# W_down's first 256 rows on 32 partitions, half by SyncE's queue and half by GpSimd's

## The chip, the core and the metric

The kernel runs on one core of one Trainium2 chip. A core has five engines with instruction streams of their own (TensorE, written PE in the profile, with PEld for its weight loads; VectorE, DVE; ScalarE, ACT; GpSimd, POOL; SyncE, SP) and 16 DMA engines that move data between HBM and the on-chip memory of 128 partitions. The metric is device time in microseconds (us) of one execution. Before the change it is 195.08 us, the median of three runs (195.07 to 195.08).

## What is computed

One decode step of a transformer block for 4 tokens: a layer norm, then attention over a window of 4096 cached positions and, beside it, a SwiGLU feed-forward network, both added to the input.

```python
xn = layernorm(x)                                    # 4 x 512
q = xn @ wq                                          # 32 heads of 128
k, v = k_cache[:, :, Sk-4096:], v_cache[:, :, Sk-4096:]   # 8 kv heads, 4 query heads share one
p = softmax(q @ k.T * 128**-0.5)
a = (p @ v) @ wo                                     # 4096 -> 512
g = silu(xn @ w_gate); u = xn @ w_up                 # 512 -> 1792
out = x + a + (g * u) @ w_down                       # 1792 -> 512
```

All tensors are bf16. The window of the two caches is 64 MiB; wq and wo are 4 MiB each; w_gate, w_up and w_down 1.75 MiB each.

## The kernel before

The work goes by kv heads: eight groups, each with one 4 MiB load of K and one of V. K and V have two buffers each (`KB`, `VB`). For a group PE transposes K in 16 chunks (L415), DVE and ACT copy the transposes out of PSUM (L326, L280), PE computes scores (L427), maxima are found and subtracted (L434, L439), ACT takes the exponential (L283), and PE multiplies by V (L448) and by ones for the softmax denominator (L454). `spin` (L470) puts idle matmuls where PE would otherwise wait.

All bulk loads go through SP's queue, in the order in which `on_sync` (L235 to L267) issues them: wq, w_gate, w_up, then K and V of each group, then W_down, then wo. A load is issued ahead of its need as soon as its buffer comes free: K of group g waits for the transposes of group g-2 (L239), V for the product with V of group g-2 (L250). Wo overwrites the first K buffer, so its five pieces (`WOS`: 16, 8, 5, 2 and 1 rows of 32 per partition) wait for the last transposes that read it (L264). A DMA queue has a ring on each DMA engine, and a load of 128 partitions is split over the 16 DMA engines, eight partitions to each.

The feed-forward part is done at both ends. At the start PE computes gate and up (L396) for F = 1792 columns in NM + NX pieces: NM = 13 pieces of 128 columns, and NX = 8 pieces that hold the first 128 columns in another split, 16 (`JX`) at a time. At the end `down` (L482) multiplies the 13 pieces of 128 rows by `WD`, and `down_rest` (L487) the 8 pieces of 16 rows by `WDX`. `WD` holds W_down's rows 128 to 1791, 13 rows to a partition. `WDX` holds rows 0 to 127 on 16 partitions, eight rows (8 KB) to a partition; it lies in the first 16 partitions of `WG`, w_gate's buffer, whose last reader is the gate product. `WDX` is loaded by four transfers (L263); transfer o writes partitions o, o+4, o+8 and o+12:

```python
wdx_ap = B_w_down[0:F - FM].rearrange("(i o m) n -> o i m n", o=4, m=NX)   # L185
eng.dma_start(WDX[o:JX:4], wdx_ap[o]).then_inc(d_wd, 16)                   # L263
```

After `down` and `down_rest`, PE adds x (L532) and multiplies by wo as its pieces land (L534 to L544); rows 0 to 15 accumulate in four column groups (L474), which ACT copies out (L298), and the rest in two (L478). DVE and ACT copy the result (L370, L300), and ACT's queue stores it (L302).

GpSimd makes constants at the start (`on_gpsimd`, L191 to L233): identity matrices, masks, and `sel`, a 128 x 32 matrix with a one where row and column agree modulo 32, made by four selections with a drain behind each of the last three (L226). It signals `s_go` (L202), for which ACT waits, and `s_const` (L233), for which PE waits, and issues no DMA.

Of the kernel before, what the change touches and what calls it, by code (L numbers as in the profile page):

```python
# [3 lines left out]
BF16 = mybir.dt.bfloat16  # L4
FP32 = mybir.dt.float32
ALU = mybir.AluOpType
# [4 lines left out]
def bass_parallel_sum__sliding_block_cached__swiglu_ffn__decode_kernel(  # L11
# [15 lines left out]
    F = B_w_gate.shape[1]  # L27
# [3 lines left out]
    NF = F // 128  # L31
# [16 lines left out]
    WOE = 16  # L48
    NR = HQ * Dh // 128

    NM = NF - 1
    FM = 128 * NM
    NX = 8
    JX = 128 // NX

    def sb(name, shape, dtype, align=32):
        return nc.alloc_sbuf_tensor(name, shape, dtype, align_bytes=align)
# [8 lines left out]
    WU = sb("wu_sb", [128, NC, F], BF16, 512)  # L66
    WD = sb("wd_sb", [128, NM, D], BF16, 512)
    WO = KB[0][:].rearrange("p t d -> p (t d)").rearrange("p (r n) -> p r n", r=NR)

    WDX = WG[0:JX].rearrange("p c f -> p (c f)")[:, 0:NX * D].rearrange("p (m n) -> p m n", n=D)  # L70
    X = sb("x_sb", [B, D], BF16, 512)
# [24 lines left out]
    S2 = sb("s2", [128, D], FP32)  # L96
    ex = sb("ex", [128, NM + NX, B], FP32)
    gs = sb("gs", [128, NM + NX, B], FP32)
    guT = sb("guT", [128, NM + NX, 32], BF16)
    ident = sb("ident", [128, 128], BF16)  # L100
# [6 lines left out]
    dq = sb("dq", [128, 4], FP32)  # L107
    dr = sb("dr", [128, NR], BF16)
    sel = sb("sel", [128, 32], FP32)
    head = sb("head", [128, 128], FP32)  # L110
    y = sb("y_sb", [B, D], BF16)

    ps = nc.alloc_psum_tensor
# [13 lines left out]
    q_ps = ps_S[0][:, 0:HQ * B]  # L127
    gate_ps = ps_O[:, 64:64 + (NM + NX) * B].rearrange("p (t b) -> p t b", b=B)
    up_ps = ps_O[:, 192:192 + (NM + NX) * B].rearrange("p (t b) -> p t b", b=B)
# [6 lines left out]
    def sem(name):  # L136
        return nc.alloc_semaphore(name=name)
# [2 lines left out]
    d_wg = sem("d_wg")  # L140
    d_wu = sem("d_wu")
    d_wd = sem("d_wd")
    d_out = sem("d_out")
    d_wo = [sem("d_wo%d" % q) for q in range(len(WOS) - 1)]
    d_k = [sem("d_k%d" % s) for s in range(2)]
# [10 lines left out]
    s_gu = sem("s_gu")  # L156
# [25 lines left out]
    wg_ap = B_w_gate.rearrange("(p c) n -> p c n", c=NC)  # L182
    wu_ap = B_w_up.rearrange("(p c) n -> p c n", c=NC)
    wd_ap = B_w_down[F - FM:F].rearrange("(p t) n -> p t n", t=NM)
    wdx_ap = B_w_down[0:F - FM].rearrange("(i o m) n -> o i m n", o=4, m=NX)  # L185
    wo_ap = A_wo.rearrange("(p r) n -> p r n", r=NR)

    def kv_ap(cache, g, a, b):
        return cache[:, g, Sk - W:, :].rearrange("b (j t) d -> j b t d", j=NJ)[:, :, a:b, :]

    def on_gpsimd(eng):  # L191
        eng.memset(ident[:], 0.0)
        eng.memset(I4[:], 0.0)
        eng.memset(st_eps[:], EPS)
        eng.memset(ones[:], 1.0)
        eng.memset(own[:], 1.0)
        eng.memset(moff[:], 0.0)
        eng.memset(coff[:], 0.0)
        eng.memset(neg[:], 0.0)
        eng.memset(dq[:], 1.0)  # L200
        eng.memset(sel[:], 0.0)
        eng.drain().then_inc(s_go, 1)  # L202

        def select(t, pattern, op, fill, base, mult):
            eng.affine_select(t, t, pattern=pattern, compare_op=op, fill=fill, base=base,
                              channel_multiplier=mult)

        def rows(n):
            select(sel[:], [[-1, 32]], ALU.not_equal, 1.0, -32 * n, 1)
        select(I4[:], [[-1, B]], ALU.not_equal, 1.0, 0, 1)  # L210
        select(ident[:], [[-1, 128]], ALU.not_equal, 1.0, 0, 1)
        select(neg[:], [[-1, NH]], ALU.not_equal, -1.0, 0, 1)
        ownv = own[:].rearrange("k (j b) -> k j b", b=B)
        moffv = moff[:].rearrange("k (j b) -> k j b", b=B)
        coffv = coff[:].rearrange("k (b h) -> k b h", h=REP)
        select(ownv, [[0, NJ], [-REP, B]], ALU.is_ge, 0.0, 0, 1)
        select(moffv, [[0, NJ], [-REP, B]], ALU.is_ge, OFF, 0, 1)
        select(coffv, [[-REP, B], [0, REP]], ALU.is_ge, OFF, 0, 1)
        select(dq[:], [[-32, 4]], ALU.is_ge, 0.0, 0, 1)
        rows(0)  # L220
        eng.drain()
        select(ownv, [[0, NJ], [REP, B]], ALU.is_ge, 0.0, REP - 1, -1)
        select(moffv, [[0, NJ], [REP, B]], ALU.is_ge, OFF, REP - 1, -1)
        select(coffv, [[REP, B], [0, REP]], ALU.is_ge, OFF, REP - 1, -1)
        select(dq[:], [[32, 4]], ALU.is_ge, 0.0, 31, -1)
        for n in range(1, 4):  # L226
            rows(n)
            eng.drain()
        eng.tensor_copy(dr[:], sel[:])
        eng.tensor_copy(head[:], sel[:, 0:1].to_broadcast([128, 128]))  # L230
        eng.memset(dsum[:], 1.0)
        eng.memset(Osb[:], 0.0)
        eng.drain().then_inc(s_const, 1)  # L233

    def on_sync(eng):  # L235
        def load(g):
            u = g % 2
            if g >= 2:
                eng.wait_ge(s_tr[NCH - 1], g - 1)  # L239
            if g < HKV - 1:  # L240
                eng.dma_start(KB[u][:], kv_ap(A_k_cache, g, 0, NT)).then_inc(d_k[u], 16)
            else:

                H = NT // 2
                eng.dma_start(KB[u][:, 0:H], kv_ap(A_k_cache, g, 0, H)).then_inc(d_k[u], 16)
                eng.dma_start(KB[u][:, H:], kv_ap(A_k_cache, g, H, NT)).then_inc(d_kh, 16)
            if g == 1:
                eng.wait_ge(s_q, 1)
            if g >= 2:
                eng.wait_ge(s_pv, g - 1)  # L250
            eng.dma_start(VB[u], kv_ap(A_v_cache, g, 0, NT)).then_inc(d_v[u], 16)

        def load_wo(n, a, b):
            eng.dma_start(WO[:, a:b, :], wo_ap[:, a:b, :]).then_inc(d_wo[n], 16)

        eng.dma_start(WQ, wq_ap).then_inc(d_wq, 16)
        eng.dma_start(WG[:], wg_ap).then_inc(d_wg, 16)
        eng.dma_start(WU[:], wu_ap).then_inc(d_wu, 16)
        for g in range(HKV):
            load(g)  # L260
        eng.dma_start(WD[:], wd_ap).then_inc(d_wd, 16)
        for o in range(4):
            eng.dma_start(WDX[o:JX:4], wdx_ap[o]).then_inc(d_wd, 16)  # L263
        eng.wait_ge(s_tr[NCH - 1], HKV - 1)  # L264
        for q in range(len(WOS) - 1):
            load_wo(q, WOS[q], WOS[q + 1])
        eng.wait_ge(d_out, 16)  # L267
# [104 lines left out]
    def on_tensor(eng):  # L372
# [100 lines left out]
        def acc4(n, left, right, start, stop):  # L473
            return mm(acc4_ps[32 * n:32 * n + 32, :], left, right, start=start, stop=stop, skip_group_check=True)  # L474
# [10 lines left out]
                acc4(t % 4, guT[:, t, :], WD[:, t, :], t < 4, False)  # L485

        def down_rest():  # L487
            for m in range(NX):
                acc4(m % 4, guT[0:JX, NM + m, :], WDX[:, m, :], False, False)

        with eng.Fori(1, HKV + 1, 2) as m:

            d = eng.snap((m - 1) * 8 + 16)
            for u in range(2):
                n = m if u == 0 else eng.snap(m + 1)
# [31 lines left out]
        for b in range(B):  # L527
            last = mm(perm_ps[b // 2][:, NR * (b % 2):NR * (b % 2 + 1)], OT[:, b, 2:HKV + 2].rearrange("p k h q -> p (k h q)"), dr[:])
        last.then_inc(s_pm, 1)
        down_rest()  # L530
        spin(2, 1)
        acc(ident[0:B, 0:B], X[:], True, False)  # L532
# [15 lines left out]


    on_sync(nc.sync)  # L550
    on_gpsimd(nc.gpsimd)
    on_scalar(nc.scalar)
    on_vector(nc.vector)
# [28 lines left out]
```

## Time and profile before

| | |
|---|---|
| median of three runs | 195.08 us |
| the profiled execution | 195.3 us |
| its span, first to last instruction | 193.9 us |
| bytes moved | 81.14 MB, mean 418 GB/s |
| PE busy (matmul) | 163.8 us |
| DVE, ACT, POOL busy | 99.0, 69.1, 5.7 us |
| mean granted TensorE clock | 0.991 |

All times of the trace are counted from the span's start. In rows of the timeline the columns are start, duration, engine (a q behind it is its sequencer or DMA queue), source line, operation, output <- inputs, shapes and count; in brackets the idle time before it and what ended that. In tables by windows, "DMA share" is the busy share of the 16 DMA engines in that stretch.

### The profile page before, as it was taken

How to read it: one execution, taken by the hardware profiler on the slowest of the kernel's cores; microseconds unless marked ns; L12 is line 12 of the kernel's file. 1: busy time of each engine (PE TensorE's matmuls, PEld its weight loads, DVE VectorE, ACT ScalarE, POOL GpSimd, SP SyncE). 2: the span in 40 equal slices, each digit the busy share in tenths (PEclk: the TensorE clock that was granted, in tenths of full speed). 3: DMA queues.
4: the chain of work that ended last, by engine and by line, in shares of the span. 5: the costliest groups of instructions: out<-in, count | busy, mean ns of one | idle time of the engine just before them, and what ended most of it. 6: DMA issues, size and time to landing. Idle time of an engine off the chain costs nothing.

```text
span 193.9 us, 6951 instructions
## 1 busy us (share of the span) xinstructions
PE 163.8 (84%) x3179; PEld 135.2 (70%) x3179; DVE 99.0 (51%) x200; ACT 69.1 (36%) x100; POOL 5.7 (3%) x33
## 2 busy tenths in 40 slices
PE   0038973998699899999999799989996999999995
PEld 0038973997389759956994699469945994997532
DVE  0200011578258737870885188428842884588230
ACT  5510000243416343525461446234623462363421
POOL 7300000000000000000000000000000000000000
PEclk9999999999789999999999999999999999999999
DMA  6999999999999999999999999999999999999993
GB/s 216 433 438 429 427 429 433 429 433 429 433 429 436 426 429 436 426 433 433 439 433 433 433 433 433 433 433 433 433 433 433 433 426 433 439 433 433 436 400 131
DMA packets 3800, 81.14 MB, mean 418 GB/s; under 512 B 440, under 2 KB 576, under 8 KB 832
## 3 DMA queue, kind: packets, MB, share of 16 engines
q1 hardware_dynamic: 3776, 81.00, 97.5%
q8 instruction: 8, 0.13, 0.2%
q10 hardware_dynamic: 16, 0.01, 0.0%
HBM read 81.01 MB, written 0.00 MB: 418 GB/s over the span
## 4 chain that ended last, share of the span: by engine, by line
PE 48%; DMA 44%; DVE 5%; issue 1%; SPq 1%; ACT 0%; DVEq 0%
DMA kbuf<-in_A_k_cache_dram 44%; PE ps_kt L415 23%; PE ps_s L427 8%; PE ps_o L448 5%; PE ps_kt L470 4%; DVE kT L326 2%; PE ps_s L439 2%; PE ps_s L464 2%; DVE mx L332 2%; PE ps_s L478 1%; PE ps_s L474 1%; PE ps_s L461 1%; PE ps_kt L454 1%; PE ps_kt L434 0%; ACT s L298 0%
## 5 line engine op out<-in xcount | busy, mean ns | idle before, releaser
L415 PE MATMUL ps_kt<-ident,kbuf 128*128 128x128 bf16 x1024 | 78.2, 224 | 9.0 <-DMA kbuf<-in_A_k_cache_dram 8.5
L415 PEld LDWEIGHTS ps_kt<-ident,kbuf 128*128 128x128 bf16 x1024 | 60.6, 100 | 11.2 <-DMA kbuf<-in_A_k_cache_dram 9.6
L326 DVE COPY kT<-ps_kt 128x1024 bf16<-128x1024 bf16 x88 | 57.6, 686 | 18.5 <-PE ps_kt L415 16.5
L280 ACT ACTIVATE kT<-ps_kt 128x1024 bf16<-128x1024 bf16 x40 | 40.9, 1023 | 52.9 <-PE ps_kt L415 52.9
L427 PE MATMUL ps_s<-qC,kT 128*128 128x16 bf16 x1024 | 44.8, 170 | 2.6 <-DVE kT L326 1.9
L427 PEld LDWEIGHTS ps_s<-qC,kT 128*128 128x128 bf16 x1024 | 38.4, 97 | 4.6 <-DVE kT L326 4.1
L283 ACT ACTIVATE p<-ps_s 128x512 bf16<-128x512 f32 x32 | 16.5, 603 | 34.0 <-PE ps_s L439 34.0
L332 DVE TENSOR_REDUCE mx<-ps_s 128x16 f32<-128x512 f32 x32 | 22.0, 689 | 6.9 <-PE ps_s L427 5.0
L470 PE MATMUL ps_kt<-own,ones 128*128 128x512 bf16 x82 | 20.7, 380 | 0.0
L448 PE MATMUL ps_o<-vbuf,p 128*32 128x256 bf16 x512 | 19.1, 289 | 0.3
L448 PEld LDWEIGHTS ps_o<-vbuf,p 128*32 128x32 bf16 x512 | 14.9, 101 | 5.9 <-ACT p L283 4.2
L343 DVE TENSOR_REDUCE dsum<-ps_kt 128x16 f32<-128x256 f32 x8 | 3.4, 425 | 28.6 <-PE ps_kt L454 28.6
L454 PE MATMUL ps_kt<-p,ones 128*32 128x256 bf16 x64 | 16.9, 287 | 0.0
L470 PEld LDWEIGHTS ps_kt<-own,ones 128*128 128x128 bf16 x82 | 6.6, 97 | 7.0 <-issue 1.1
L377 PE MATMUL ps_s<-i,xn 4*128 4x4 f32 x4 | 0.6, 254 | 10.1 <-DVE xn L312 10.1
L439 PE MATMUL ps_s<-cm,own 128*128 128x512 bf16 x32 | 8.3, 380 | 1.0 <-DVE cm L340 1.0
L377 PEld LDWEIGHTS ps_s<-i,xn 4*128 4x128 f32 x4 | 0.6, 208 | 10.1 <-issue 10.1
L454 PEld LDWEIGHTS ps_kt<-p,ones 128*32 128x32 bf16 x64 | 6.6, 103 | 0.1
L290 ACT ACTIVATE ex<-ps_o 128x84 f32<-128x84 f32 x1 | 0.2, 240 | 17.5 <-PE ps_o L396 17.5
L439 PEld LDWEIGHTS ps_s<-cm,own 128*128 128x128 bf16 x32 | 2.5, 97 | 5.3 <-DVE cm L340 3.4
L286 ACT ACTIVATE osb<-ps_o 128x256 f32<-128x256 f32 x8 | 3.1, 383 | 8.2 <-PE ps_kt L454 8.2
L464 PE MATMUL ps_s<-sel,osb 128*128 128x16 f32 x36 | 5.8, 275 | 0.0
(83 smaller groups left out, 84.8 us busy)
## 6 DMA issues: line engine op xcount, KB each, us to landing
vbuf<-in_A_v_cache_dram SPq DMA_DIRECT2D x8, 4096.0 KB, 30.5
kbuf<-in_A_k_cache_dram SPq DMA_DIRECT2D x7, 4096.0 KB, 27.4
vbuf<-in_A_wq_dram SPq DMA_DIRECT2D x1, 4096.0 KB, 12.4
kbuf<-in_A_k_cache_dram SPq DMA_DIRECT2D x2, 2048.0 KB, 25.3
kbuf<-in_A_wo_dram SPq DMA_DIRECT2D x1, 2048.0 KB, 27.2
wg_sb<-in_B_w_gate_dram SPq DMA_DIRECT2D x1, 1792.0 KB, 16.1
wu_sb<-in_B_w_up_dram SPq DMA_DIRECT2D x1, 1792.0 KB, 20.9
wd_sb<-in_B_w_down_dram SPq DMA_DIRECT2D x1, 1664.0 KB
```

The source lines that it names most:

```text
L280: eng.activation(KT[:, c % 4], kt_ps[c % 3], ACT.Copy).then_inc(s_ev[c], 1)
L283: eng.activation(P[:, BT * q:BT * (q + 1), :], ps_S[q][:].rearrange("p (t n) -> p t n", n=NH), ACT.Exp, scale=SCALE).then_inc(s_p[q], 1)
L326: eng.tensor_copy(KT[:, c % 4], kt_ps[c % 3]).then_inc(s_ev[c], 1)
L332: eng.tensor_reduce(mx[:, q, :], ps_S[q][:].rearrange("p (t n) -> p n t", n=NH), AX.X, ALU.max)
L343: eng.tensor_reduce(dsum[:], den_ps.rearrange("p (t n) -> p n t", n=NH), AX.X, ALU.add).then_inc(s_dn, 1)
L415: last = eng.transpose(kt_ps[c % 3][:, k, :], KB[u][:, CH * c + k, :], ident[:])
L427: last = mm(ps_S[q][:, NH * t:NH * (t + 1)], KT[:, c % 4, k, :], QC[:], start=(t == 0), stop=False, skip_group_check=True)
L439: mm(ps_S[q][:].rearrange("p (t n) -> p t n", n=NH), own[:], CM[:].unsqueeze(1).to_broadcast([128, BT, NH]), start=False, stop=True, skip_ ...
L448: mm(O_ps[32 * n:32 * n + 32, :], P[:, t:t + 2, :].rearrange("p t n -> p (t n)"), VB[u][:, t:t + 2, :].rearrange("p t d -> p (t d)"), star ...
L454: last = mm(den_ps[32 * n:32 * n + 32, :], ones[:, 0:32], P[:, DT * e:DT * (e + 1), :].rearrange("p t n -> p (t n)"), start=(e < 4), stop= ...
L464: last = mm(O2_ps, Osb[:, Dh * h:Dh * (h + 1)], sel[:, NH * h:NH * (h + 1)], start=(h == 0), stop=(h == 1), skip_group_check=True)
L470: mm(ps_kt[k][:], ones[:], own[:].unsqueeze(1).to_broadcast([128, 4, 128]), skip_group_check=True)
```

## The change

W_down's first 256 rows, not the first 128, are taken out of the 128-partition tile. `WD` has 12 rows to a partition and `WDX` 32 partitions with eight rows each. SP's four transfers load `WDX`'s partitions 0 to 15, now four neighbouring partitions each (0 to 3, 4 to 7, and so on); four transfers on GpSimd's queue load partitions 16 to 31 in the same way. Ahead of each of these GpSimd issues a transfer of twelve short rows, each of two pieces of 32 bytes, into a tile `pad` that nothing reads. GpSimd issues its eight transfers once the gate and up products are done (`s_gu`), because `WDX` lies in w_gate's buffer, and PE waits for all eight (`d_wx`) ahead of `down_rest`. `sel` is made by two additions of halves of the identity matrix instead of a memset and four selections.

```diff
-    NM = NF - 1
+    NM = NF - 2
     FM = 128 * NM
     NX = 8
-    JX = 128 // NX
+    JX = 256 // NX
...
+    sel2 = sb("sel2", [128, 64], FP32)
     head = sb("head", [128, 128], FP32)
+    pad = sb("pad", [12, 4, 2, 16], BF16)
...
-    wdx_ap = B_w_down[0:F - FM].rearrange("(i o m) n -> o i m n", o=4, m=NX)
+
+    wdx_ap = B_w_down[0:F - FM].rearrange("(o i m) n -> o i m n", i=4, m=NX)
...
-        eng.memset(sel[:], 0.0)
         eng.drain().then_inc(s_go, 1)
...
-        rows(0)
-        eng.drain()
+        eng.drain()
+
+        eng.tensor_tensor(sel2[:], ident[:, 0:64], ident[:, 64:128], ALU.add)
...
-        for n in range(1, 4):
-            rows(n)
-            eng.drain()
+        eng.drain()
+        eng.tensor_tensor(sel[:], sel2[:, 0:32], sel2[:, 32:64], ALU.add)
+        eng.drain()
...
         eng.drain().then_inc(s_const, 1)
+
+
+        eng.wait_ge(s_gu, 1)
+        for o in range(4):
+            with nc.allow_non_contiguous_dma(reason="short rows"):
+                eng.dma_start(pad[:, o], B_w_down[0:12].rearrange("p (a n) -> p a n", a=16)[:, 0:2, 0:16]).then_inc(d_wx, 16)
+            eng.dma_start(WDX[16 + 4 * o:20 + 4 * o], wdx_ap[4 + o], max_dma_last_dim=4096).then_inc(d_wx, 16)
...
         for o in range(4):
-            eng.dma_start(WDX[o:JX:4], wdx_ap[o]).then_inc(d_wd, 16)
+            eng.dma_start(WDX[4 * o:4 * o + 4], wdx_ap[o]).then_inc(d_wd, 16)
...
         def down_rest():
+            eng.wait_ge(d_wx, 128)
             for m in range(NX):
                 acc4(m % 4, guT[0:JX, NM + m, :], WDX[:, m, :], False, False)
```

More of the change, by code (lines that the diff above doesn't have):

```diff
@@ L142, in bass_parallel_sum__sliding_block_cached__swiglu_ffn__decode_kernel @@
     d_wd = sem("d_wd")
+    d_wx = sem("d_wx")
     d_out = sem("d_out")
@@ L206, in select @@
                               channel_multiplier=mult)
-        def rows(n):
-            select(sel[:], [[-1, 32]], ALU.not_equal, 1.0, -32 * n, 1)
         select(I4[:], [[-1, B]], ALU.not_equal, 1.0, 0, 1)
```

## The prediction, made before the change was run

> **What bounds the kernel now.** I read the page first: span, DMA rates, queues, chain.
>
> ```profile
> span 193.9 us, 6951 instructions
> ...
> GB/s 216 433 438 429 427 429 433 429 433 429 433 429 436 426 429 436 426 433 433 439 433 433 433 433 433 433 433 433 433 433 433 433 426 433 439 433 433 436 400 131
> ...
> q1 hardware_dynamic: 3776, 81.00, 97.5%
> q8 instruction: 8, 0.13, 0.2%
> ...
> PE 48%; DMA 44%; DVE 5%; issue 1%; SPq 1%; ACT 0%; DVEq 0%
> ```
>
> From the second slice to the last but two the DMA engines move 433 GB/s, which is 27.1 GB/s for each of the 16; q1, SP's queue, keeps them busy 97.5% of the whole span. The chain of waits is half PE, half DMA, so its last stretch decides.
>
> ```profile
> 120.96 28.01 DMA kbuf<-in_A_k_cache_dram
> 148.97 0.05 issue
> 149.01 1.51 PE ps_kt L415 x24
> ...
> 185.49 0.97 PE ps_s L474 x13
> ...
> 186.65 0.54 PE ps_s L474 x8
> ...
> 187.93 1.01 PE ps_s L474 x16
> 188.94 0.02 issue
> 188.96 0.60 ACT s L298
> 189.57 0.04 issue
> 189.61 2.54 PE ps_s L478 x36
> 192.15 0.02 issue
> 192.17 0.41 DVE y_sb L370
> ```
>
> K of the seventh group lands at 148.97. From there PE works through two groups, W_down and wo without a wait for a DMA, up to the last product, L478. How close DMA is at that point stands in the timeline of weight loads, and in wo's issues and landings:
>
> ```profile
> 189.83 1.51 PEld L478 LDWEIGHTS ps_s<-kbuf,oP 128*4 128x4 bf16 x26
> 191.51 0.09 PEld L478 LDWEIGHTS ps_s<-kbuf,oP 128*4 128x4 bf16 x4 [0.18 <-DMA kbuf<-in_A_wo_dram]
> 191.85 0.08 PEld L478 LDWEIGHTS ps_s<-kbuf,oP 128*4 128x4 bf16 x2 [0.25 <-DMA kbuf<-in_A_wo_dram]
> ```
> ```profile
> L254 SPq DMA_DIRECT2D kbuf<-in_A_wo_dram x5: 335/432/434, 159.7 to 161.5; - x5
> ...
> DMA to landing us min/median/max: 27.2/30.3/30.5
> ```
>
> The last piece of wo is issued at 161.5 and lands some 30.3 later, at 191.8, and PE's last two loads start at 191.85. So the end follows the DMA engine that finishes last: later by x, and the kernel is later by x; earlier, and PE gains at most the two waits, 0.18 + 0.25 = 0.43 us. How the 16 engines finish is read from the DMA share by windows (the last two columns are DMA share and GB/s):
>
> ```profile
> 189.50:190.00 0.50, 0.39 (x4) 0.19 (x6) 0.00 (x0) 0.06 (x1) 0.00 (x0) 1.00 0.80 324
> 190.00:190.50 0.50, 0.50 (x12) 0.38 (x10) 0.00 (x0) 0.00 (x0) 0.00 (x0) 1.00 0.76 297
> 190.50:191.00 0.50, 0.50 (x14) 0.34 (x10) 0.00 (x0) 0.00 (x0) 0.00 (x0) 1.00 0.68 242
> 191.00:191.50 0.50, 0.50 (x12) 0.28 (x9) 0.00 (x0) 0.00 (x0) 0.00 (x0) 1.00 0.14 47
> 191.50:192.00 0.50, 0.50 (x10) 0.17 (x6) 0.00 (x0) 0.00 (x0) 0.00 (x0) 1.00 0.00 0
> ```
>
> A share of 0.76 is 12 engines of 16. Four engines are out of work from about 189.7; eleven stop near 191.0; the 0.14 after it is about one engine, which runs to the end at 191.5 (its data has landed by 191.8). So there are three numbers: four engines have about 1.2 us to spare, eleven about 0.4, one nothing.
>
> **The change part by part.** *Bytes taken from all engines.* W_down in the DMA issues:
>
> ```profile
> wd_sb<-in_B_w_down_dram SPq DMA_DIRECT2D x1, 1664.0 KB
> ...
> wg_sb<-in_B_w_down_dram SPq DMA_DIRECT2D x4, 32.0 KB
> ```
>
> The 128-partition tile loses one row of 13, 128 KB, or 8 KB for each engine: 8192 B / 27.1 GB/s = 0.30 us earlier for all, the last one included. This is the whole possible gain on the DMA side.
>
> *Bytes given to a few.* Four 32 KB transfers of 8 KB rows come back on GpSimd's queue: if one engine serves the same row of each, four engines get 32 KB more, 1.21 us, which is just what the idle four have to spare. When they run matters little: the queue in front of every engine is never empty, so 1.21 us at 25 us is still 1.21 us at the end.
>
> The Trainium skill (DMA: Bandwidth & Descriptors, the section on why a DMA increments its semaphore by 16) says that a transfer of four rows runs on four engines: from SP's queue on the lowest-numbered four, from GpSimd's on the next four of a cursor that goes round all 16. By that rule twelve rows and then four return the cursor to its place, and all four transfers fall on one set of engines. No row of the profile names engines, so whether that set is the idle one can't be read here.
>
> *The layout of the rows.* SP's four transfers are as many and as large as before, but each now writes four neighbouring partitions instead of four that lie four apart. No sustained transfer to neighbours alone is in this trace. Everything that runs at the full rate is spread evenly: eight partitions to an engine and 27.1 GB/s to eight partitions. Lower bound of a transfer's cost: as now, 8 KB on each of four engines side by side, 0.30 us, 1.21 for the four. Upper bound: its four partitions take together no more than the rate that eight are ever seen to take, 32 KB / 27.1 GB/s = 1.21 us, 4.84 for the four: 3.63 us lost on four engines. In between, engines that are out of step pass through the four places one behind the other, 4 + 3 = 7 turns of 0.30, 2.1 us in all. The last windows show engines up to a microsecond out of step, so I take a value nearer to that end, ten turns, 3.0 us, 1.8 lost. The eight packets of instructions on q8 and the four engines that W_down's short transfers use now make twelve, the number that is busy at the end; so I count these four among the eleven, with 0.4 us to spare: 1.8 - 0.4 = +1.4 us at the end, ahead of the terms that all engines share.
>
> The same question holds for GpSimd's four transfers, and there another engine is writing its own eight partitions at the full rate all the time. Lower bound: 1.21 us for the four engines, all of it spare. Upper bound: five writers on one place, 8 KB at 27.1 / 5 GB/s, 1.51 us a transfer, 6.0 in all, of which 1.2 + 0.4 us is free: +4.4; and the engine whose place it is loses 1.21, of which it has 0 to 0.4 to spare. I take the same +1.4; it falls on other engines, so the two aren't added.
>
> The Trainium skill (SBUF — State Buffer, "Door 1: The DMA port swizzle") gives these places a name: partitions 0 to 3 share one of 16 write ports with 32 to 35, and it lists 27.6 GB/s for a transfer to partitions 0 to 3 alone. By that rule the upper bound would hold, with 4.8 us for SP's four transfers; the layout before met four ports with every transfer. It is the rule that speaks most against the change; no run here shows it yet.
>
> *The short rows.* Nothing like them is in the trace. Below: nothing. Above: each piece as dear as 1 KB, 0.04 us at 27.1 GB/s, two pieces for an engine and four times, 0.3 us. I take 0.1, late for twelve engines.
>
> *GpSimd.* Four selections and a memset go, two additions come, all before `s_const`.
>
> ```profile
> 1.56 0.11 POOL L201 MEMSET sel<- 128x32 f32 x1
> ...
> 6.93 0.31 POOL L232 MEMSET osb<- 128x256 f32 x1
> ...
> 10.11 0.61 PE L377 MATMUL ps_s<-i,xn 4*128 4x4 f32 x4 [10.11 <-DVE xn L312]
> ```
> ```profile
> L205 POOL TENSOR_SCALAR_AFFINE_SELECT sel<-sel 128x32 f32<-128x32 f32 x4 | 0.8, 207 | 0.4 <-issue 0.4
> ```
>
> GpSimd is done at 7.24, and PE's first matmul waits for xn until 10.11: 2.9 us of cover, and about 0.9 us of work goes. Worth nothing. Uncovered, the two additions would cost some 0.5 us by the rows of selections. The eight transfers have no row on this queue; SP's take:
>
> ```profile
> L263 SPq DMA_DIRECT2D wg_sb<-in_B_w_down_dram x4: 577/605/730, 148.4 to 150.5; - x4
> ```
>
> Between nothing and, if ten times as long as SP's 0.6 us, 48 us for eight, they would still be issued by 73, with nothing queued behind them on GpSimd, and `down_rest` asks for them at 186.65. The new wait on PE ends long before; behind it stand only `down_rest` and wo. SP issues as many transfers as before.
>
> *PE.* Gate and up have 20 pieces instead of 21, eight matmuls fewer:
>
> ```profile
> 17.43 5.19 PE L396 MATMUL ps_o<-xnT,wg_sb 128*128 128x4 bf16 x84 [0.57 <-DMA wg_sb<-in_B_w_gate_dram]
> ...
> 2.18 30.22 DMA kbuf<-in_A_k_cache_dram
> ```
>
> At 62 ns each that is 0.5 us, hidden by the wait for the first K, which lands at 32.40. `down` has 12 matmuls for 13, 0.97 / 13 = 0.07 us of PE's own chain, which matters only where DMA isn't the last. `down_rest` keeps eight.
>
> The sum, against the span of 193.9 us: -0.30 + 0.1 + 1.4 = **+1.2 us**, with PE's 0.07 under the DMA, so a span of 195.1. The profiled execution lasted 195.3 us, 1.4 around its span, and is 0.2 above the median; the difference goes onto the median of 195.08: **196.3 us**.
>
> **The rivals.** *As planned* (not slower): neighbours cost nothing and the twelve-row transfers steer the four large ones onto the idle engines. For it: 12 of 16 engines busy at the end, and 1.21 us that fits the gap of 1.2. Against it: nothing in the profile says which engines idle. Time: -0.30 + 0.1 = -0.2, 194.9 us. Even with free short rows and PE's 0.07 counted, -0.30 - 0.07 = -0.37, or 194.71, is the most that rows bear out.
>
> *The wrong engines* (slower): the transfers land on four of the twelve without spare time. If each of the eight packets of instructions held up another engine, half of the 16 are late whatever W_down does, and a set of four chosen blind meets a late one more often than not. +1.21 - 0.30 + 0.1 = +1.0 if the last engine is hit, 0.4 less if another: 195.7 to 196.1, say 195.9 us.
>
> *It doesn't do what it says*: the twelve-row transfers don't steer, and the four large ones fall on four different sets of engines. Then each engine gets back the 8 KB that it lost: 0 + 0.1, 195.2 us.
>
> **How the numbers follow.** My forecast (neighbours share a place) has 0.42, the wrong engines 0.24, as planned 0.26, no steering 0.08. With 0.2% of 195.08, 0.39 us, as about what a measurement of this kernel can tell from no change, slower (above 195.47) is 0.42 + 0.24 = 0.66; faster (below 194.69) I give 0.08 out of the planned case, for a gain beyond the rows; within is 0.18 + 0.08 = 0.26. The likeliest case alone runs from 195.4 (seven turns: 0.9 - 0.4 - 0.2 = +0.3) to 198.1 (3.63 - 0.4 - 0.2 = +3.0), and to 199.3 by GpSimd's upper bound. The range for all reaches down into the planned case and leaves out the faster tail: 194.7; above, it leaves out the extremes of sharing: 198.0.
>
> **What would show it.** Neighbours sharing: W_down's landing spreads out, the DMA share falls to about 0.8 or less right after W_down's tile, and in the last windows four engines run alone for a microsecond or more, a share near 0.25. As planned: the share stays near 1 until about 190.6 and falls at once, and wo's last landing is 0.2 earlier. Wrong engines: two steps at the end, with four engines still idle early. No steering: the present windows 0.1 later. GpSimd's transfers should appear on a queue of their own between 24 and 40 us. I am wrong if the last landing of wo is not later, or if it is later while no engine is slow in W_down.

## The result

The changed kernel is slower: 197.70 us, the median of six runs (196.75 to 197.95), against 195.10 us (195.07 to 195.20) for the kernel before on the same chip. The ratio is 1.0124, with a 95% interval of 1.0104 to 1.0145, or +2.0 to +2.8 us. The direction was forecast; the size is twice the +1.2 us of the sum. The changed kernel's own spread, 1.2 us, is nine times that of the kernel before.

### The profile page after: what moved, and what is told of

Its sections match the earlier page's. It is cut to its first block, busy times and chain, and to the rows that moved or that the text cites. A ratio compares the mean times of both kernels' runs of the same rounds, so it can differ in the third digit from the quotient of the medians.

```text
span 196.0 us, 6933 instructions
## 1 busy us (share of the span) xinstructions
PE 164.5 (84%) x3170; PEld 134.9 (69%) x3170; DVE 98.9 (50%) x200; ACT 69.1 (35%) x100; POOL 10.2 (5%) x38
## 4 chain that ended last, share of the span: by engine, by line
PE 48%; DMA 43%; DVE 5%; issue 1%; SPq 1%; ACT 0%; DVEq 0%
DMA kbuf<-in_A_k_cache_dram 43%; PE ps_kt L423 23%; PE ps_s L435 8%; PE ps_kt L478 5%; PE ps_o L456 5%; DVE kT L334 2%; PE ps_s L447 2%; PE ps_s L472 2%; DVE mx L340 2%; PE ps_s L486 1%; PE ps_s L469 1%; PE ps_s L482 1%; PE ps_kt L462 1%; PE ps_kt L442 0%; ACT s L306 0%
## 5 line engine op out<-in xcount | busy, mean ns | idle before, releaser
L423 PEld LDWEIGHTS ps_kt<-ident,kbuf 128*128 128x128 bf16 x1024 | 60.6, 100 | 10.5 <-DMA kbuf<-in_A_k_cache_dram 9.5
L478 PE MATMUL ps_kt<-own,ones 128*128 128x512 bf16 x82 | 22.2, 400 | 0.0
```

The lines of the kernel that those rows point to most:

```text
L423: last = eng.transpose(kt_ps[c % 3][:, k, :], KB[u][:, CH * c + k, :], ident[:])
L478: mm(ps_kt[k][:], ones[:], own[:].unsqueeze(1).to_broadcast([128, 4, 128]), skip_group_check=True)
```

## The profile after

The profiled execution lasted 197.38 us with a span of 196.0 us; 1.4 us lie around the span, as before. First the page: span, DMA rate in 40 slices, and queues.

```profile
span 196.0 us, 6933 instructions
...
GB/s 214 429 439 428 434 458 435 428 411 422 413 415 445 421 425 431 435 435 435 428 428 428 428 435 428 428 435 428 435 441 435 425 418 451 445 418 392 420 395 67
...
q1 hardware_dynamic: 3776, 80.87, 96.8%
q0 software_dynamic: 320, 0.14, 0.3%
q8 instruction: 8, 0.13, 0.3%
```

SP's queue moves 0.13 MB less and GpSimd's queue, q0, moves that. But four slices in a row, the ninth to the twelfth (39 to 59 us), drop to 411 to 422 GB/s, where the kernel before had 429 to 433. That is where GpSimd's transfers run. Its transfers in the timeline, and in the DMA issues of 28 to 60 us (the last figure is the median time from issue to landing):

```profile
28.14 0.71 POOL L240 DMA_DIRECT2D pad<-in_B_w_down_dram  x1 [21.38 <-PE ps_o L404]
28.84 0.60 POOL L241 DMA_DIRECT2D wg_sb<-in_B_w_down_dram  x1
...
32.33 0.59 POOL L241 DMA_DIRECT2D wg_sb<-in_B_w_down_dram  x1
```
```profile
wg_sb<-in_B_w_down_dram POOLq DMA_DIRECT2D x4, 32.0 KB, 17.3
```

The chain of waits has the shape that it had before, with everything from the seventh group's K on 2.1 us later:

```profile
123.08 28.01 DMA kbuf<-in_A_k_cache_dram
151.09 0.05 issue
151.14 1.51 PE ps_kt L423 x24
...
191.73 2.50 PE ps_s L486 x36
194.23 0.02 issue
194.25 0.41 DVE y_sb L378
```

That K landed at 148.97 before and lands at 151.09 now. W_down's bulk and SP's small transfers are issued only after 149 us, so the whole 2.1 us are lost before SP's part of the change runs. The last weight loads still wait for wo's last two pieces, for 0.17 and 0.23 us:

```profile
191.94 1.51 PEld L486 LDWEIGHTS ps_s<-kbuf,oP 128*4 128x4 bf16 x26
193.62 0.09 PEld L486 LDWEIGHTS ps_s<-kbuf,oP 128*4 128x4 bf16 x4 [0.17 <-DMA kbuf<-in_A_wo_dram]
193.94 0.08 PEld L486 LDWEIGHTS ps_s<-kbuf,oP 128*4 128x4 bf16 x2 [0.23 <-DMA kbuf<-in_A_wo_dram]
```

These waits are worth less than they look. The last product takes 2.54 us before and 2.50 here; in e4_strided (below), where no weight load waits for wo, its line of the chain is

```profile
191.87 2.36 PE ps_s L486 x36
```

So wo adds 0.14 us here and 0.18 before. The rest of the end is set earlier: from the landing of the seventh group's K to the end of that product PE has 43.0 us of work of its own (e4_strided, f1_own, f4_turn, g1_less and g2_short), and it takes 43.1 us here and 43.2 before. Two things can thus hold the end, the last DMA engine at that K and the last one at wo, and in both kernels they lie within 0.2 us of each other.

How the 16 engines finish now (windows; DMA share and GB/s last):

```profile
190.50:191.00 0.50, 0.50 (x12) 0.03 (x4) 0.00 (x0) 0.00 (x0) 0.00 (x0) 1.00 0.92 365
191.00:191.50 0.50, 0.02 (x4) 0.00 (x0) 0.00 (x0) 0.42 (x1) 0.00 (x0) 1.00 0.76 289
...
192.00:192.50 0.50, 0.50 (x12) 0.32 (x10) 0.00 (x0) 0.00 (x0) 0.00 (x0) 1.00 0.33 129
192.50:193.00 0.50, 0.50 (x14) 0.36 (x9) 0.00 (x0) 0.00 (x0) 0.00 (x0) 1.00 0.21 80
193.00:193.50 0.50, 0.50 (x14) 0.40 (x10) 0.00 (x0) 0.00 (x0) 0.00 (x0) 1.00 0.13 47
```

Before, the share fell in one step, from 0.68 to 0.14. Now it falls in small steps: about five engines (0.33 of 16) still work at 192 us, two at 193. The load is less even than before.

The landing of a DMA is the last of 16 completions, one for each engine. The trace holds all 16, though without the engines' names. For the load of K of group 7, in us:

```
               mean    the 16 completions in order
before        147.81   146.9 147.0 147.1 147.1 147.1 147.1 147.1 147.2 | 148.4 148.4 148.4 148.5 148.5 148.6 148.7 149.0
after         148.91   147.3 147.4 147.4 147.5 147.7 | 148.4 148.5 148.9 148.9 148.9 149.1 | 149.9 150.3 150.6 151.0 151.1
```

Before, eight engines are early and eight late by some 1.5 us. The eight packets of q8 fit the eight: the first two run at 18.7 and 25.7 us, and of the completions of group 1's K two are late (32.3 and 32.4 against 31.4 for the next). In the loads that land last at 43, 52, 62, 72 and 81 us three, four, five, seven and eight completions are late, as many as packets of q8 have run in time for them, and eight in every load of K and V after that. So a 16 KB packet of instructions seems to set one engine back by some 1.5 us (the early eight have a mean of 147.06, the late eight of 148.56), two and a half times the 0.6 us of its bytes; no run takes such a packet away. After the change the mean is 1.10 us later, although GpSimd's 128 KB are worth only 0.30 us for each of 16 engines. The mean differs little from one execution to the next: the five kernels that put nothing on GpSimd's queue have 147.78 to 147.89.

## The experiments

Theory G: the loss is in GpSimd's large transfers, which fall on engines without spare time and write partitions that other engines are writing. Rivals: L, the forecast's main term (SP's four transfers to neighbouring partitions); S, GpSimd's queue, its short rows and its completions; R, reading W_down's rows in 8 KB pieces. Times are medians beside the kernel before on the same chip; K7 is the mean of the 16 completions above (before: 147.81).

| kernel | time, before | ratio (95%) | K7 |
|---|---|---|---|
| after | 197.70, 195.10 | 1.0124 (1.0104 to 1.0145) | 148.91 |
| e1_layout | 196.05, 195.19 | 1.0043 (1.0031 to 1.0056) | 147.84 |
| e2_pads | 195.82, 195.19 | 1.0030 (1.0018 to 1.0043) | 147.94 |
| e3_nopads | 196.87, 195.19 | 1.0098 (1.0077 to 1.0118) | 149.17 |
| e4_strided | 197.39, 195.19 | 1.0117 (1.0100 to 1.0134) | 149.52 |
| f1_own | 196.25, 195.13 | 1.0059 (1.0042 to 1.0076) | 148.23 |
| f2_src | 197.73, 195.13 | 1.0139 (1.0101 to 1.0177) | 149.86 |
| f3_sp | 197.40, 195.13 | 1.0142 (1.0098 to 1.0187) | 147.78 |
| f4_turn | 195.96, 195.13 | 1.0046 (1.0032 to 1.0060) | 148.28 |
| g1_less | 194.99, 195.18 | 0.9994 (0.9984 to 1.0003) | 147.89 |
| g2_short | 195.11, 195.18 | 0.9995 (0.9985 to 1.0004) | 147.91 |
| g3_read | 195.11, 195.18 | 0.9999 (0.9989 to 1.0008) | 147.86 |
| h1_third | 196.13, 195.19 | 1.0048 (1.0032 to 1.0065) | 148.29 |

### Which part of the change costs

**e1_layout**, the kernel before with SP's transfers to neighbours:

```diff
-    wdx_ap = B_w_down[0:F - FM].rearrange("(i o m) n -> o i m n", o=4, m=NX)
+    wdx_ap = B_w_down[0:F - FM].rearrange("(o i m) n -> o i m n", i=4, m=NX)
...
-            eng.dma_start(WDX[o:JX:4], wdx_ap[o]).then_inc(d_wd, 16)
+            eng.dma_start(WDX[4 * o:4 * o + 4], wdx_ap[o]).then_inc(d_wd, 16)
```

> The kernel before, with one edit: SP's four transfers write four neighbouring partitions each instead of four that lie four apart. In the changed kernel the last landing of K of the second pair of groups (at 73 us, long before W_down is loaded) is already 2.1 us late, so theory G (the loss is GpSimd's transfers) expects 0 to +0.4 us here, since these four engines have some 0.4 us to spare. Theory L (the forecast: neighbours in SP's transfers) expects +0.8 to +2.4 us.

+0.8 us, at the edge of theory L and above what G allowed: the layout alone does cost, and it costs all engines. The 16 completions of wo's first piece run from 185.4 to 187.6 us, against 184.9 to 186.8 before; their mean is 0.7 us later, and the earliest engine, one of the idle four, lost 0.5 us as well.

**e2_pads**, the kernel before with the short rows alone on GpSimd's queue:

```diff
         eng.drain().then_inc(s_const, 1)
+        eng.wait_ge(s_gu, 1)
+        for o in range(4):
+            with nc.allow_non_contiguous_dma(reason="short rows"):
+                eng.dma_start(pad[:, o], B_w_down[0:12].rearrange("p (a n) -> p a n", a=16)[:, 0:2, 0:16]).then_inc(d_wx, 16)
...
         def down_rest():
+            eng.wait_ge(d_wx, 64)
```

> The kernel before, with GpSimd's four transfers of twelve short rows alone, and PE's wait for them; W_down is loaded as before. Theory G (the large transfers cost) expects +0.1 to +0.5 us, the short rows and their completions. Theory S (GpSimd's queue itself costs: its short rows, its completions) expects +1.5 to +2.5 us.

+0.6 us, just above theory G's range and far below theory S's, and misleading by itself: the profiled execution lasted 195.88 us with a span of 193.9 us, the span of the kernel before. The lost time lies outside the span, 2.0 us around it instead of 1.4, and the trace's DMA records differ in one point there: one more packet of instructions, behind the last instruction of the program.

```
queue  start us  ns   bytes
14     195.65    549  8192    (e2_pads; the kernel before and the changed one have none after the start)
```

**e3_nopads**, the changed kernel without the short rows:

```diff
         for o in range(4):
-            with nc.allow_non_contiguous_dma(reason="short rows"):
-                eng.dma_start(pad[:, o], ...).then_inc(d_wx, 16)
             eng.dma_start(WDX[16 + 4 * o:20 + 4 * o], wdx_ap[4 + o], max_dma_last_dim=4096).then_inc(d_wx, 16)
```

> The changed kernel without the four transfers of short rows, so that nothing steers the four large ones. If the loss comes from all four falling on one set of engines without spare time, it is now spread over four sets, 0.3 us each: -0.1 to +0.5 us against before. If it comes from four neighbouring partitions being written at once beside another engine's stream, whatever engines write them, it stays at +1.2 us or more.

+1.7 us by the medians: the loss stays without the steering, so it isn't only that all four fall on one set of engines.

**e4_strided**, the changed kernel with all small transfers four partitions apart:

```diff
-    wdx_ap = B_w_down[0:F - FM].rearrange("(o i m) n -> o i m n", i=4, m=NX)
+    wdx_ap = B_w_down[0:F - FM].rearrange("(h i o m) n -> h o i m n", h=2, o=4, m=NX)
...
-            eng.dma_start(WDX[16 + 4 * o:20 + 4 * o], wdx_ap[4 + o], max_dma_last_dim=4096).then_inc(d_wx, 16)
+            eng.dma_start(WDX[16 + o:32:4], wdx_ap[1, o], max_dma_last_dim=4096).then_inc(d_wx, 16)
...
-            eng.dma_start(WDX[4 * o:4 * o + 4], wdx_ap[o]).then_inc(d_wd, 16)
+            eng.dma_start(WDX[o:16:4], wdx_ap[0, o]).then_inc(d_wd, 16)
```

> The changed kernel with every small transfer, SP's and GpSimd's, writing four partitions that lie four apart, as SP's did before. If four writers on one place are the loss, it falls to the price of the wrong engines: +0.7 to +1.2 us against before, or to -0.2 if the engines are the idle ones. If the loss is the choice of engines and the short rows alone, nothing changes: +2.1 to +2.6 us.

+2.2 us: as much as the changed kernel within the intervals. But the edit changes two layouts at once, and the trace shows them pulling apart. For GpSimd's transfers the neighbours were the better layout: K7 is 0.6 us later here than in the changed kernel (149.52 against 148.91), so four writers on one place aren't the point there. For SP's transfers they were the worse one, as in e1_layout. Windows of the changed kernel, then of e4_strided:

```profile
180.00:182.00 2.00, 1.74 (x16) 0.80 (x16) 1.16 (x4) 0.00 (x0) 0.00 (x0) 1.00 1.02 358
```
```profile
180.00:182.00 2.00, 1.74 (x20) 0.74 (x16) 1.28 (x3) 0.00 (x0) 0.00 (x0) 1.00 0.96 408
```

The last engine at K of group 7 is equally late in both (151.1 and 151.2 us), and so is the end. What was left of theory G was the choice of engines, and theory P: that partitions 16 to 31, however they are dealt out, are being written by other engines at the same time. Theory Q is S for the large transfers: GpSimd's queue costs wherever it writes.

### Whose partitions are written

**f1_own** takes e4_strided and sends GpSimd's rows to partitions 80 to 95; **f2_src** takes it and reads from elsewhere; **f3_sp** takes it and moves GpSimd's transfers to SP's queue; **f4_turn** takes it and turns the engines:

```diff
# f1_own (WGX is the same view of w_gate's buffer as WDX, on all 128 partitions)
-            eng.dma_start(WDX[16 + o:32:4], wdx_ap[1, o], max_dma_last_dim=4096).then_inc(d_wx, 16)
+            eng.dma_start(WGX[80 + o:96:4], wdx_ap[1, o], max_dma_last_dim=4096).then_inc(d_wx, 16)
# f2_src
+            eng.dma_start(WDX[16 + o:32:4], A_k_cache[0, 0, 0:512].rearrange("(i q m t) d -> q i m (t d)", i=4, q=4, t=4)[o], ...)
# f3_sp (GpSimd's eight transfers taken out)
+        for o in range(4):
+            eng.dma_start(WDX[16 + o:32:4], wdx_ap[1, o]).then_inc(d_wd, 16)
# f4_turn (in the loop: a first transfer of 4 short rows, then 12; one of 8 at the end)
+            r = 4 if o == 0 else 12
+                eng.dma_start(pad[0:r, o], B_w_down[0:r]...).then_inc(d_wx, 16)
...
+            eng.dma_start(pad[0:8, 4], B_w_down[0:8]...).then_inc(d_wx, 16)
```

> e4_strided with one edit: GpSimd's four large transfers write partitions 80 to 95 (four apart) of w_gate's buffer instead of 16 to 31, so W_down's rows 128 to 255 are not where the product reads them, which multiplies by what w_gate left there. In e4_strided the third load of K into the first buffer landed 1.8 us later on the mean of its 16 completions than in the kernel before (72.07 against 70.31 us), while the bytes of the four transfers are worth 0.30 us a DMA engine. Theory P (a DMA engine that writes partitions which another engine is writing at the time holds up all of them): if GpSimd's transfers run on the engines that carry partitions 80 to 95 in a full load, the mean is +0.3 to +0.6 and the time +1.0 us against before or less. Theory Q (the queue itself, its 4 KB pieces and its completions, costs wherever it writes): mean +1.2 to +1.8 and +1.8 to +2.4 us, as in e4_strided. It stays there by theory P too if they run on other engines.

> e4_strided with one edit: GpSimd's four large transfers read 128 KB from a part of the K cache outside the window instead of W_down's rows 128 to 255, so these rows are missing from the product. Theory R (reading W_down's rows in 8 KB pieces holds up the other reads) expects the loss to shrink, to +1.2 us against before or less. Theories P and Q expect no change: +1.8 to +2.4 us.

> e4_strided without GpSimd's transfers: SP issues all eight small transfers, four apart each, behind the 128-partition tile; the four on partitions 16 to 31 run on the same engines as the first four. If sharing partitions with another engine's stream costs as on GpSimd's queue (theory P), the tail is late for all engines by more than a microsecond: +1.2 to +2.2 us. If the queue is the cost (theory Q), only these engines' extra 32 KB count: 1.21 - 0.30, of which 0 to 0.4 spare: +0.4 to +0.9 us.

> e4_strided with one edit: the first transfer of short rows has 4 rows and not 12, and a fifth one of 8 rows follows at the end, so that the four large ones should fall eight engines further round, on those that carry partitions 16 to 31 in a full load and therefore write their own. The output is complete. Theory P expects the slowing of all engines to vanish here (mean of that load of K +0.3 to +0.6) and a time of -0.2 to 0 us against before if these four are the idle ones, +0.6 to +1.2 if they are late ones. Theory Q expects +1.8 to +2.4 us.

The windows of 28 to 60 us tell them apart; the last two columns are the share of time in which the DMA engines have a packet in work, and GB/s. Before, after, e4_strided, f1_own, f4_turn, in this order:

```profile
28.00:60.00 32.00, 25.04 (x445) 22.80 (x446) 17.35 (x36) 9.71 (x14) 0.00 (x0) 0.95 1.02 439
```
```profile
28.00:60.00 32.00, 24.88 (x443) 22.66 (x444) 17.21 (x35) 9.56 (x14) 4.78 (x8) 0.95 1.02 426
```
```profile
28.00:60.00 32.00, 25.01 (x434) 22.78 (x435) 16.91 (x35) 9.14 (x13) 4.78 (x8) 0.95 1.02 417
```
```profile
28.00:60.00 32.00, 24.97 (x434) 22.82 (x435) 16.92 (x35) 9.19 (x14) 4.79 (x8) 0.95 1.03 439
```
```profile
28.00:60.00 32.00, 24.99 (x458) 22.44 (x459) 17.66 (x36) 9.76 (x14) 5.42 (x9) 0.95 1.02 437
```

The share is the same 1.02 or 1.03 everywhere: the engines look equally busy, and only the bytes tell. 426 and 417 GB/s where GpSimd's rows go to partitions 16 to 31 from one set of engines; 439 and 437 where either the partitions or the engines are changed. So neither the queue nor partitions 16 to 31 cost by themselves: the pairing does. In time, f1_own is +1.1 us, 0.1 more than theory P allowed, and f4_turn +0.8, within its range.

The trace's DMA records show where the time goes. SP's packets of 32 KB take 1.213 us each when nothing disturbs them. Of those that start between 28 and 60 us, 423 of 427 take no longer than that in the kernel before, 418 of 423 in f1_own and 409 of 421 in f4_turn, but 234 of 410 in the changed kernel and 174 of 402 in e4_strided. The time above 1.213 us adds up to 1.2 us in f1_own, 10.5 after and 20.2 in e4_strided. Shared out over 16 engines, e4_strided loses 1.2 us more than f1_own by this and the changed kernel 0.6; their K7 is later by 1.29 and 0.68. So the loss lies in SP's own packets, which take longer. The reader should take from this that a busy share can't show a transfer that is held up inside its packets.

The Trainium skill (DMA: Bandwidth & Descriptors, the section on why a DMA increments its semaphore by 16, and the descriptor swizzle) numbers the engines so that GpSimd's four, if its cursor stands at 0 at the start, would be 12 to 15, which carry partitions 80 to 95 in a full load, and after the turn 4 to 7, which carry 16 to 31. f1_own and f4_turn agree: the slowing goes in both. The Trainium skill's rule of ports (SBUF — State Buffer, "Door 1: The DMA port swizzle") agrees on which pairings are bad. By the port's rate alone four carriers and four owners would lose up to 1.21 us each, an estimate of 0.6 us for the mean of 16 engines; the price measured here is twice that.

Measured, e4_strided's K7 is 1.24 us above f4_turn's (149.52 against 148.28), and its earliest completion moved from 147.2 to 148.2 us, so engines that take no part in the pairing lose a microsecond too. Why it spreads to them isn't shown.

Reading other memory (f2_src) changed nothing for the better, +2.6 us: theory R falls here. SP's queue with the same pairing (f3_sp) is as bad, +2.3 us, of which the bytes alone explain 0.4 to 0.9; so theory Q falls. There the loss lies in the tail (K7 is 147.78). Windows of f3_sp:

```profile
180.00:182.00 2.00, 1.96 (x24) 0.78 (x24) 0.43 (x2) 1.01 (x3) 0.00 (x0) 1.00 1.27 377
182.00:184.00 2.00, 2.00 (x70) 1.53 (x58) 0.11 (x1) 1.16 (x4) 0.00 (x0) 1.00 0.82 274
```

For the same windows the kernel before has:

```profile
180.00:182.00 2.00, 1.97 (x13) 0.67 (x15) 0.63 (x3) 0.74 (x2) 0.00 (x0) 1.00 1.05 445
182.00:184.00 2.00, 2.00 (x72) 1.69 (x72) 0.00 (x0) 1.33 (x3) 0.00 (x0) 1.00 0.97 418
```

### Which engines are late, and the small terms

**h1_third** is f4_turn turned four engines further (a first transfer of 8 short rows, a last one of 4), writing partitions 64 to 79:

```diff
-            r = 4 if o == 0 else 12
+            r = 8 if o == 0 else 12
...
-            eng.dma_start(WDX[16 + o:32:4], wdx_ap[1, o], max_dma_last_dim=4096).then_inc(d_wx, 16)
+            eng.dma_start(WGX[64 + o:80:4], wdx_ap[1, o], max_dma_last_dim=4096).then_inc(d_wx, 16)
```

> f4_turn with the large transfers turned four engines further, by a first transfer of 8 short rows and a last one of 4, and writing partitions 64 to 79, four apart; W_down's rows 128 to 255 are therefore not where the product reads them. In f1_own three of the four engines were late already, in f4_turn two. The kernel before has eight early engines at 147 us: four that SP's transfers use, one of f1_own's set, two of f4_turn's. That leaves one early engine for this set: three engines in the last group of completions, and +0.9 to +1.2 us against before. If this is the set of the idle four, no engine stands apart at the end and the time is -0.2 to 0 us against before.

+0.9 us and three engines apart. The completions of K of group 7 for the three sets:

```
               mean    the 16 completions in order
f1_own        148.23   147.1 147.1 147.2 147.2 147.3 147.4 147.4 | 148.5 148.5 148.6 148.6 148.7 148.7 | 149.8 149.9 149.9
f4_turn       148.28   147.2 147.2 147.3 147.3 147.4 147.4 148.2 148.5 148.6 148.6 148.7 148.7 148.7 148.8 | 149.8 150.1
h1_third      148.29   147.0 147.1 147.1 147.2 147.3 147.4 147.4 | 148.5 148.6 148.6 148.7 148.8 148.9 | 150.0 150.0 150.0
```

All three means are 0.4 to 0.5 us above before: the 0.30 us of the bytes and a little for the short rows. The engines that were late and now carry 32 KB more stand apart at the end: three, two and three, all eight late ones. So none of the three sets of four is the idle one, if the late engines are the same in each execution; the four idle engines are spread over them, one, two and one. Each of these kernels pays about a microsecond for that. The tail of f4_turn shows it as two engines that go on alone for a microsecond (share 0.12 is two of 16):

```profile
191.00:191.50 0.50, 0.50 (x12) 0.32 (x10) 0.00 (x0) 0.00 (x0) 0.00 (x0) 1.00 0.14 51
191.50:192.00 0.50, 0.50 (x14) 0.43 (x10) 0.00 (x0) 0.00 (x0) 0.00 (x0) 1.00 0.12 45
192.00:192.50 0.50, 0.50 (x14) 0.42 (x10) 0.00 (x0) 0.00 (x0) 0.00 (x0) 1.00 0.05 16
```

**g1_less** is e4_strided with nothing on GpSimd's queue; **g2_short** adds the short rows alone to it; **g3_read** is the kernel before with e1_layout's order of reading and its own order of writing:

```diff
# g1_less (and PE's wait for d_wx is taken out)
-        eng.wait_ge(s_gu, 1)
-        for o in range(4):
-            ...
# g2_short
-            eng.dma_start(WDX[16 + o:32:4], wdx_ap[1, o], max_dma_last_dim=4096).then_inc(d_wx, 16)
# g3_read
-    wdx_ap = B_w_down[0:F - FM].rearrange("(i o m) n -> o i m n", o=4, m=NX)
+    wdx_ap = B_w_down[0:F - FM].rearrange("(o i m) n -> o i m n", i=4, m=NX)
```

> e4_strided without anything on GpSimd's queue: the 128-partition tile has 12 rows of W_down to a partition, SP's four transfers load rows 0 to 127, and rows 128 to 255 are not loaded at all, so they are missing from the product. It measures the one gain of the change by itself: 8 KB less for every DMA engine, -0.30 us, with up to 0.07 more from PE's one matmul less: 194.7 to 194.9 us. If PE's own chain holds the end instead, 0 to -0.1 us.

> g1_less with GpSimd's four transfers of short rows and PE's wait for them; rows 128 to 255 of W_down are again missing. In e2_pads the span didn't change, and a packet of 8 KB of instructions came after it, at 195.65 us, which the kernel before doesn't have. If that packet made e2_pads' +0.6 us, this kernel, whose GpSimd program is shorter, is within 0.15 us of g1_less. If the short rows cost, it is 0.4 to 0.7 us above it.

> The kernel before, whose four small transfers read 8 KB pieces that lie side by side in HBM, as in e1_layout, but still write partitions four apart, as before; the rows of these 128 land on other partitions than the product takes them for. e1_layout was +0.8 us. If writing four neighbouring partitions is its cause (theory P), this is within 0.15 us of before. If reading neighbouring pieces is, it is +0.6 to +0.9 us.

The gain term by itself is 0.1 to 0.2 us (ratio 0.9994, which the interval doesn't part from no change); wo's last piece lands at 191.4 us instead of 191.8, and PE no longer waits for it, but K of group 7 lands no earlier (148.9 against 149.0) and PE's 43.0 us behind it hold the end. The short rows cost nothing that the times can tell, which leaves the packet of instructions as the likely difference in e2_pads. And g3_read is within 0.1 us of before, so e1_layout's loss isn't in the reading: it is in four engines writing one group of neighbours. Windows of e1_layout, then of g3_read:

```profile
180.00:182.00 2.00, 1.97 (x20) 0.79 (x22) 0.47 (x2) 0.97 (x2) 0.00 (x0) 1.00 1.06 332
```
```profile
180.00:182.00 2.00, 1.97 (x20) 0.78 (x22) 0.45 (x2) 0.99 (x3) 0.00 (x0) 1.00 1.07 455
```

332 GB/s against 455, at the same share.

No version beats the kernel before. One with GpSimd's rows on exactly the four idle engines, which don't lie side by side, wasn't tried; g1_less bounds what it could bring at some 0.2 us.

## Why the prediction was right in direction and half the size

A chain of runs from the kernel before to the changed one splits the loss; its steps add up to the whole by construction. In us against the kernel before: 8 KB less for each engine, with the short rows, -0.1 (g2_short); engines without spare time +1.0 (f4_turn less g2_short: 1.0046 - 0.9995 = 0.0051 of 195); two engines writing the same partitions +1.4 (e4_strided less f4_turn: 0.0071); neighbours instead of four apart about +0.1 (after less e4_strided, inside the intervals). Together +2.4. With f1_own in f4_turn's place, whose large transfers run on the same engines as e4_strided's, the two middle steps are +1.2 and +1.1.

- *What bounds the kernel* held in the main: a DMA engine that is late makes the end late, and wo's last landing moved with the end, 191.8 to 193.9 us. But the prediction looked at wo alone. The late engine already counts at K of the seventh group, which is 2.1 us later, and PE's 43.0 us of work behind it lead to the same end within 0.2 us.
- *Bytes taken from all engines*, -0.30: half of it or less shows in the time (g1_less). PE's two waits of 0.18 and 0.25 us were not 0.43 to gain but 0.18, since without them the last product takes 2.36 us instead of 2.54.
- *GpSimd's transfers*: this is the step that failed. "I take the same +1.4; it falls on other engines, so the two aren't added", with "of which 1.2 + 0.4 us is free": it priced the sharing for four engines that had time to spare, and left GpSimd's transfers hidden behind SP's. The runs show +2.4 for them (e4_strided less g2_short: 1.0117 - 0.9995 = 0.0122), for two reasons that the prediction kept apart and that add: the engines were mostly late ones (the rival of the wrong engines, +1.0 forecast, +1.0 to +1.2 measured), and sharing partitions cost another +1.1 to +1.4 on top.
- *The price of sharing* was worked out for the writers and the owner alone. It falls on all 16 engines: e4_strided's earliest completion is a microsecond late.
- *The layout of SP's rows* was the main term of the sum, +1.4. Alone it is +0.8 (e1_layout), and not as four engines that fall behind: all 16 lose 0.5 to 0.8 us. In the changed kernel it slows the stage as well (358 GB/s against 408), but there the late K has already set the end and each engine has 8 KB less to load, so PE loses 0.14 us to wo, where it loses nothing in e4_strided, and no more. That the direction came out right is therefore partly luck: the term that gave the sum its sign was worth some 0.1 us in the changed kernel, and the loss came from the transfers that the sum left out.
- *The short rows*, 0.1: no more than that. *GpSimd's constants*: hidden, as said. The row of the last one in the timeline of the changed kernel ends at 6.77 us, half a microsecond sooner:

```profile
6.45 0.32 POOL L233 MEMSET osb<- 128x256 f32 x1
```

- *The new wait of PE* ended early, as said, by far: issued from 28 us, the large transfers landed some 17 us later. The guess of 24 to 40 us for them was too short, as their 32 pieces of 4 KB ran from 35.5 to 56.2 us. They share the engines with SP's packets of 1.213 us each; that they queue behind these is likely, not shown.
- *What would show it*: the steps at the end came as for the wrong engines. The low rate behind W_down's tile came as for neighbours, but in GB/s (358); the DMA share, which was to fall to 0.8, stayed at 1.02. The test "I am wrong if ... it is later while no engine is slow in W_down" named the wrong place: W_down's second half is loaded at 35 to 58 us, and that is where the engines were slow.

## What to carry to other kernels

A small transfer that fills up idle DMA engines should write partitions that those same engines carry in the large loads around it; otherwise two engines write one place, and every engine pays, at a busy share that looks unchanged, so compare GB/s and not the share. Before rows are given to "idle" engines, read the 16 completions of a load that lands late in the kernel: idle engines need not lie side by side, and a transfer that needs four in a row can meet a late one, as all three sets did here. When two rivals would hurt in different places, ask whether they exclude each other before taking the larger alone.

## What was not expected of the hardware

- A 16 KB packet of instructions seems to set one engine back by some 1.5 us, two and a half times the time of its bytes at 27.1 GB/s. The number of late completions grows with the packets of q8, from two at 32 us to eight at 81, which fits eight packets on eight different engines; half of the engines are late from then on.
- Transfers of 32 KB to partitions that another engine is writing slow all 16 engines: 417 GB/s instead of 437 for 32 us (e4_strided, f4_turn), in packets of 32 KB that take up to 1.5 us instead of 1.213. Four engines that write four neighbouring partitions do the same: 332 GB/s instead of 455 for 2 us (e1_layout, g3_read). The cause of the spread to uninvolved engines is not shown by these runs.
- In e2_pads an 8 KB packet of instructions comes after the last instruction, and some 0.6 us that the span doesn't contain. g2_short, which issues the same short rows from a GpSimd program with fewer selections, has neither; what brings the packet isn't shown further.
